# Between two layers of a fused attention and two-layer gated network: another order for the last down products, the first up products and the work beside them

## The chip, the cores and the metric

One core of a Trainium2 chip runs the whole program. TensorE (PE in the rows; its weight loads are PEld) does the matmuls, VectorE (DVE) and ScalarE (ACT) read the PSUM banks and do the elementwise work, GpSimd (POOL) does a little elementwise work in SBUF, and SyncE (SP) issues the DMAs. The metric is the time of one execution in device microseconds.

## The reference, cut to what matters

```python
x = attention(q, k, v)                  # 1536 tokens x 512
h = x @ moe_w_in                        # 512 -> 2048
x = (h * cos(h)) @ moe_w_out            # first layer, 2048 -> 512
h = x @ moe2_w_in
sp = log1p(exp(h))
out = (h * tanh(sp)) @ moe2_w_out       # second layer (the Mish gate)
```

The four weights come as 64-bit floats, and the kernel narrows them itself with integer operations.

## The kernel before, in words

Every fp32 operand of a layer's matmul is held as a high and a low part, and one 128-deep piece of a product takes three matmuls (high x high, high x low, low x high). All matmuls of the layers are 128x128 by 128x512. Tokens are three blocks j = 0, 1, 2 of 512. The output of the first layer is accumulated in ACC tiles; its two parts go to the tiles X (xh and xl), from which the second layer reads.

**First layer.** It walks over 12 stages: four groups of hidden columns times three token blocks. A stage has four up products of 12 matmuls (L180) and four down products `down(s, u)`, u = 0 to 3, of 12 matmuls (L585). Stages are numbered from 0, so stage 11 is the last one, block j = 2. A down product lands in a PSUM bank; its `add` (DVE, L594) adds the bank to ACC, which frees the bank. In the last group its `end` follows: ACT casts the high part into xh (L598) and POOL subtracts it for the low part xl (L599). Down products rotate over banks 3, 4 and 5 in this stretch.

**Between the layers** the code writes the order out by hand. Engines take their instructions in the order of the code, each waiting for what it needs.
- `do_downs(k)` issues up to two down products that are due by k. `head(k, pe)` issues the product `pe`, then the ends of the downs of the head before last, then the adds of all downs issued so far, then the low parts of gates (`later`).
- `first(f, j, bank)` is an up product of group 0 of the second layer: 12 matmuls (L698) over X of block j, first u = 0, 1, then u = 2, 3. Six of them exist, f = 0, 1 times j = 0, 1, 2.
- `gated(...)` is ACT's Mish from the bank (L675) and ACT's cast of the high part (L668); the low part (DVE, L669) comes with the next unit.
- `tsum(i, part)`, i = 0 to 3, makes sums of token blocks from ACC for the later groups (which compute some products by sums of blocks): part 0 is the sum (DVE, L737), part 1 the high part (ACT, L756), part 2 the low part (DVE, L737). They are 128x1024, or two of 128x512. `tsum(3, 1)` and `tsum(3, 2)` overwrite X of block 1, u = 0, 1.
- `chunk(h, c, ...)` narrows and splits one 128x512 weight piece: x (ACT, L123), a, b, c (DVE, L127, L130, L133), s the high part (ACT, L141), l the low part (DVE, L144). `wsums(1, p)` makes sums of the weights of group 1: parts 0 to 3 on DVE (L156), 4 on ACT (two, L162), 5 on DVE (two, L164). `wload` (L108) issues the DMA of a piece into one of two staging buffers, and waits for `c` of the piece that was there.
- `down2(0, j, u)` is a down product of group 0 of the second layer: 6 matmuls (L713). Its bank goes to ACC by an ACT copy (L723). In order, down2(0, 0, 0) has bank 4, then 5, 6, 3, and for j = 1: 4, 7, 5, 3.
- `unit(pe, post, side)` issues `pe`, then `side`, then the waiting low parts of gates, then `post`.

After that stretch a loop runs over the groups h = 1 to 7; its first product (`m1`) is six matmuls of L698.

In the kernel before the order of PE in this stretch is: first(0,0), first(1,0), down(11,0), down(11,1), first(0,1), down(11,2), first(1,1), down(11,3), four down2 of j = 0, first(0,2), one down2 of j = 1, first(1,2), three down2 of j = 1, then the loop. The first layer's last stage but one ends with down(10,3), just ahead of it.

Of the kernel before, what the change touches and what calls it, by code (L numbers as in the profile page):

```python
# [20 lines left out]
def kernel(  # L21
# [78 lines left out]
    def wload(l, g, c):  # L100
        st = wst.tile([128, 512], I64 if wide else F32, tag="wst", name="wst")
        if l == 0:
            src, r = wsrc[0][c // KD], 128 * (c % KD)
            ap = src[r:r + 128, g * GW:(g + 1) * GW] if c < KD else src[g * GW + r:g * GW + r + 128, :]
            nc.sync.dma_start(out=st, in_=ap)
        elif c < 2:
            ap = wsrc[1][0][256 * c:256 * c + 256, g * HW:(g + 1) * HW].rearrange("(k p) n -> p k n", p=128)
            nc.sync.dma_start(out=st.rearrange("p (k n) -> p k n", k=2), in_=ap)  # L108
        else:
            r = g * HW + 128 * (c - 2)  # L110
            nc.sync.dma_start(out=st, in_=wsrc[1][1][r:r + 128, :])
        wstage[l, g, c] = st
# [422 lines left out]
    def layers():  # L535
        with ExitStack() as es:
# [42 lines left out]
            def down(s, u):  # L579
                l, g, j = stages[s]  # L580
                ps = dbank()[:, 0:TB]
                mm = [(SLOT[4 * (g % 2) + 2 + a][:, 512 * f + 128 * u:512 * f + 128 * u + 128], G[s, f][e])
                      for f in range(GF) for a, e in PASS]
                for n, (x, y) in enumerate(mm):
                    nc.tensor.matmul(ps, lhsT=x, rhs=y, start=(n == 0), stop=(n == len(mm) - 1))  # L585
                if u == 0 and g == 0:
                    ACC[l, j] = ap.tile([128, KD * TB], F32, tag="acc", name="acc")
                acc = ACC[l, j][:, TB * u:TB * u + TB]

                def add():  # L590
                    if g == 0:
                        nc.scalar.copy(acc, ps)
                    else:
                        nc.vector.tensor_tensor(out=acc, in0=acc, in1=ps, op=ALU.add)  # L594

                def end():
                    hi, lo = (y[:, u, TB * j:TB * j + TB] for y in X)
                    nc.scalar.copy(hi, acc)  # L598
                    nc.gpsimd.tensor_tensor(out=lo, in0=acc, in1=hi.bitcast(F32), op=ALU.subtract)  # L599

                return [add, end] if g == NG - 1 else [add]

# [11 lines left out]
            def do_downs(k):  # L614

                for _ in range(2):
                    if downs and downs[0][0] <= k:
                        add, *end = down(*downs.pop(0)[1:])
                        adds.append(add)
                        ends[1].extend(end)  # L620
# [50 lines left out]
            def gated(h, f, j, ps, plus=None):  # L671
                g = tmp("gg")
                if plus is not None:
                    nc.vector.tensor_tensor(out=g, in0=ps, in1=plus, op=ALU.add)  # L674
                nc.scalar.activation(out=g, in_=ps if plus is None else g, func=AF.Mish)  # L675
                keep(h, f, j, g)
# [27 lines left out]
            def down2(h, j, u, d0=0, d1=DM, side=()):  # L704
                w = SLOT[slots(h)[1]]
                stay = (j, u) in STAY
                ps = (BANK[STAY[j, u]] if stay else dbank())[:, 0:d1 - d0]
                mm = [(G[1, h, f, j][a][:, 128 * u:128 * u + 128], w[:, 1024 * e + 512 * f + d0:1024 * e + 512 * f + d1])
                      for f in range(HG) for a, e in PASS]

                def pe():
                    for n, (x, y) in enumerate(mm):
                        nc.tensor.matmul(ps, lhsT=x, rhs=y, start=(n == 0 and (h == 0 or not stay)),  # L713
                                         stop=(n == len(mm) - 1 and (h == NH - 1 or not stay)))

                def post():
                    if u == 0 and h == 0:
                        ACC[1, j] = ap.tile([128, KD * TB], F32, tag="acc", name="acc")
                    acc = ACC[1, j][:, DM * u + d0:DM * u + d1]
                    if stay and h < NH - 1:  # L720
                        return
                    if h == 0 or stay:
                        nc.scalar.copy(acc, ps)  # L723
                    else:
                        nc.vector.tensor_tensor(out=acc, in0=acc, in1=ps, op=ALU.add)  # L725
                    if h == NH - 1:
                        r0 = TB * j + 128 * u
                        nc.sync.dma_start(out=out[r0:r0 + 128, d0:d1], in_=acc)

                unit(pe, post, side)  # L730
# [10 lines left out]
            def tsum(i, part):  # L741

                x, y = (ACC[0, j].rearrange("p (r n) -> p r n", r=2) for j in range(2))
                at, u, v = ((x[:, 0], y[:, 0], x[:, 0]), (y[:, 1], y[:, 1], x[:, 0]),
                            (y[:, 0], y[:, 1], y[:, 0]), (x[:, 1], x[:, 1], y[:, 1]))[i]
                if part == 0:
                    sub(at, u, v)
                    return
                dst = [(at, DST[i])]
                if i == 2:  # L750
                    dst = [(at[:, TB * k:TB * k + TB], GS[8 + k]) for k in range(2)]
                elif i == 3:
                    dst = [(at.rearrange("p (k n) -> p k n", k=2), DST[i])]
                for f, (hi, lo) in dst:
                    if part == 1:
                        nc.scalar.copy(hi, f)  # L756
                    else:
                        sub(lo, f, hi.bitcast(F32))

            def w(fn, *a):  # L760
                return lambda: fn(*a)

            def chunk(h, c, *parts):

                return [w(wnarrow, 1, h, c, "xabc".index(p)) if p in "xabc" else w(wsplit, 1, h, c, "sl".index(p))
                        for p in parts]

            def head(k, pe=None):

                if pe:  # L770
                    pe()
                now = later[:]
                later.clear()
                do_ends()
                g = cos_gate(*st.pop(k - 1)) if k - 1 in st else None
                do_adds()
                if g is not None:
                    made(k, k - 1, split(g))
                for op in now:
                    op()  # L780

            def first(f, j, bank):
                return lambda: plain(0, f, j, BANK[bank])

            for c in range(2):
                wload(1, 1, c)
            do_downs(NT1)
            head(NT1, first(0, 0, 0))
            gate.update(n=0, of=8)
            gated(0, 0, 0, BANK[0])  # L790
            head(NT1 + 1, first(1, 0, 1))
            tsum(0, 0)
            tsum(0, 1)
            gated(0, 1, 0, BANK[1])
            do_downs(NT1 + 1)
            head(NT1 + 2)
            tsum(2, 0)
            tsum(2, 1)
            for op in chunk(1, 0, *"xabcs"):
                op()  # L800
            do_downs(NT1 + 2)
            head(NT1 + 3, first(0, 1, 2))
            tsum(1, 0)
            tsum(0, 2)
            gated(0, 0, 1, BANK[2])
            for op in chunk(1, 0, "l") + chunk(1, 1, "x", "a", "b"):
                op()
            do_downs(NT1 + 3)
            head(NT1 + 4, first(1, 1, 0))
            tsum(3, 0)  # L810
            tsum(2, 2)
            gated(0, 1, 1, BANK[0])
            tsum(3, 1)
            for op in chunk(1, 1, "c", "s"):
                op()
            do_downs(NT1 + 4)
            head(NT1 + 5)
            tsum(1, 1)
            tsum(3, 2)
            down2(0, 0, 0, side=[w(tsum, 1, 2)])  # L820
            down2(0, 0, 1, side=chunk(1, 1, "l"))
            head(NT1 + 6)
            down2(0, 0, 2, side=[w(wsums, 1, 0, tmp), w(wsums, 1, 1, tmp)])
            down2(0, 0, 3, side=[w(wsums, 1, 2, tmp), w(wsums, 1, 3, tmp), w(wsums, 1, 4, tmp)])
            unit(first(0, 2, 1), w(gated, 0, 0, 2, BANK[1]), [w(wsums, 1, 5, tmp)])
            down2(0, 1, 0)
            wload(1, 2, 0)
            unit(first(1, 2, 2), w(gated, 0, 1, 2, BANK[2]))
            down2(0, 1, 1)
            wload(1, 2, 1)  # L830
            down2(0, 1, 2)
            down2(0, 1, 3, side=chunk(2, 0, "x"))

            for h in range(1, NH):
# [116 lines left out]
```

## Time and profile before

| | |
|---|---|
| median of 3 runs | 632.39 us (631.22 to 634.14) |
| the profiled execution | 632.21 us, its span 630.5 us |
| PE busy | 618.8 us, 98% of the span, 3048 matmuls |
| DVE busy | 505.2 us, 80% |
| ACT busy | 337.9 us, 54% |
| POOL busy | 104.4 us, 17% |
| granted TensorE clock | 1.00 over the span |

The span is the part of the time that the profiler sees; 1.7 us lie around it. Times in rows are microseconds from the span's start. The last products of the first layer begin at about 354 us, and the loop of the second layer begins at 402.75 us. In rows of the timeline the duration of a matmul (0.39) overlaps the next one's start; the distance of starts is what a matmul costs.

### The profile page before, as it was taken

The numbers are of one execution on the slowest core, as the hardware profiler recorded it, in microseconds if no ns is written. First come the engines' busy times: TensorE is split into PE (matmuls) and PEld (weight loads), VectorE is DVE, ScalarE is ACT, GpSimd is POOL, SyncE is SP. The second block draws the span as 40 slices with busy tenths as digits, with TensorE's granted clock in tenths as the row PEclk, the third lists the DMA queues.
The fourth block names the chain that finished last, engine by engine and source line by source line (L and its number), as shares of the span: only waits on it lengthen the run. The fifth ranks groups of instructions, "written<-read, shape, count | busy, mean of one in ns | idle before, by whom it ended". The sixth has DMA issues, their size and how long they took to land.

```text
span 630.5 us, 8778 instructions
## 1 busy us (share of the span) xinstructions
PE 618.8 (98%) x3048; PEld 504.8 (80%) x3049; DVE 505.2 (80%) x1036; ACT 337.9 (54%) x727; POOL 104.4 (17%) x196
## 2 busy tenths in 40 slices
PE   9899999999999999999999997999999999999998
PEld 4678778888888888888888885888888888888886
DVE  4699886599789888888889969577888888888653
ACT  4699887567555444444455464554444444444330
POOL 4588967000000000000002225000000000000000
PEclk9999999999999999999999999999999999999999
DMA  9979842021232111112111101113131313031004
GB/s 186 194 177 231 170 117 68 1 67 68 68 105 97 55 57 58 65 67 69 67 68 51 50 19 49 34 34 101 33 101 33 101 33 101 33 101 35 0 18 183
DMA packets 56458, 49.88 MB, mean 79 GB/s; under 512 B 44270, under 2 KB 44526, under 8 KB 56174
## 3 DMA queue, kind: packets, MB, share of 16 engines
q1 hardware_dynamic: 56414, 49.32, 27.8%
q8 instruction: 24, 0.39, 0.3%
q14 instruction: 20, 0.16, 0.1%
HBM read 45.57 MB, written 3.15 MB: 77 GB/s over the span
## 4 chain that ended last, share of the span: by engine, by line
PE 87%; POOL 5%; DVE 2%; ACT 2%; DMA 2%; issue 1%; SPq 1%; POOLq 0%; ACTq 0%
PE bank L180 21%; PE bank L713 20%; PE bank L585 19%; PE bank L698 18%; PE bank L251 10%; POOL pn L251 3%; DMA vn<-in_v_dram 2%; POOL vb L251 1%; DVE acc L737 1%; POOL xl L599 1%; POOL ws L144 1%; ACT gg L675 0%; DVE gl L669 0%; ACT gh L668 0%; DVE ws L144 0%
## 5 line engine op out<-in xcount | busy, mean ns | idle before, releaser
L180 PE MATMUL bank<-xh,ws 128*128 128x512 f32 x384 | 127.0, 392 | 0.0
L585 PE MATMUL bank<-gh,ws 128*128 128x512 f32 x384 | 125.7, 390 | 0.0
L713 PE MATMUL bank<-ws,gh 128*128 128x512 f32 (+1 forms) x388 | 118.9, 388 | 1.4 <-DVE acc L594 1.4
L698 PE MATMUL bank<-xh,ws 128*128 128x512 f32 x272 | 91.5, 390 | 0.0
L713 PEld LDWEIGHTS bank<-ws,gh 128*128 128x128 f32 x388 | 72.5, 188 | 17.1 <-DVE acc L594 2.3
L180 PEld LDWEIGHTS bank<-xh,ws 128*128 128x128 f32 x384 | 72.1, 188 | 15.6 <-DVE gg L569 0.7
L585 PEld LDWEIGHTS bank<-gh,ws 128*128 128x128 f32 x384 | 72.1, 188 | 15.0
L561 ACT ACTIVATE n<-bank,b_quarter 128x512 int32<-128x512 f32 x48 | 32.9, 686 | 79.7 <-PE bank L180 79.6
L713 PE MATMUL bank<-ws,gl 128*128 128x512 f32 (+1 forms) x194 | 75.2, 388 | 0.0
L180 PE MATMUL bank<-xl,ws 128*128 128x512 f32 x192 | 74.8, 390 | 0.0
L585 PE MATMUL bank<-gl,ws 128*128 128x512 f32 x192 | 74.8, 390 | 0.0
L141 ACT CAST ws<-wx 128x512 fp32r<-128x512 f32 x64 | 39.7, 621 | 51.3 <-DVE wx L133 51.1
L599 POOL TENSOR_TENSOR xl<-acc,xh 128x512 fp32r<-128x512 f32 x12 | 21.0, 1758 | 264.5 <-ACT xh L598 257.5
L669 DVE TENSOR_TENSOR gl<-gg,gh 128x512 fp32r<-128x512 f32 x48 | 33.2, 692 | 37.7 <-ACT gh L668 37.7
L698 PEld LDWEIGHTS bank<-xh,ws 128*128 128x128 f32 x272 | 51.1, 188 | 10.5
L251 POOL TENSOR_TENSOR pn<-pb,rs 128x256 f32<-128x256 f32 (+3 forms) x120 | 53.8, 470 | 18.7 <-ACT pb L251 6.2
L698 PE MATMUL bank<-xl,ws 128*128 128x512 f32 x136 | 53.2, 391 | 2.1 <-POOL xl L599 2.1
L725 DVE TENSOR_TENSOR acc<-acc,bank 128x512 f32<-128x512 f32 (+1 forms) x71 | 47.4, 674 | 8.5 <-PE bank L713 8.5
L562 DVE SCALAR_TENSOR_TENSOR r<-n,bank 128x512 f32<-128x512 int32 x48 | 32.9, 685 | 22.9 <-ACT n L561 22.9
L133 DVE SCALAR_TENSOR_TENSOR wx<-wst,wx 128x512 int32<-128x512 int32 x64 | 45.0, 704 | 1.5
L130 DVE SCALAR_TENSOR_TENSOR wx<-wst,wx 128x512 int32<-128x512 int32 x64 | 44.6, 697 | 1.9
L675 ACT ACTIVATE gg<-gg 128x512 f32<-128x512 f32 x28 | 17.7, 633 | 51.2 <-DVE gg L674 51.2
(100 smaller groups left out, 1092.2 us busy)
## 6 DMA issues: line engine op xcount, KB each, us to landing
wst<-in_moe_w_in_dram SPq DMA_DIRECT2D x32, 512.0 KB
wst<-in_moe_w_out_dram SPq DMA_DIRECT2D x32, 512.0 KB
kn<-in_k_dram SPq DMA_DIRECT2D x16, 192.0 KB
qn<-in_q_dram SPq DMA_DIRECT2D x16, 192.0 KB
vn<-in_v_dram SPq DMA_DIRECT2D x16, 192.0 KB
out_dram<-acc SPq DMA_DIRECT2D x11, 256.0 KB
vb<-in_v_dram SPq DMA_DIRECT2D x2, 960.0 KB
vt<-in_v_dram SPq DMA_DIRECT2D x32, 18.8 KB
```

The lines of the kernel that those rows point to most:

```text
L130: nc.vector.scalar_tensor_tensor(out=xi, in0=word[:, :, 0], scalar=29, in1=xi, op0=ALU.logical_shift_right, op1=ALU.bitwise_or)
L133: nc.vector.scalar_tensor_tensor(out=xi, in0=word[:, :, 1], scalar=-2 ** 31, in1=xi, op0=ALU.bitwise_and, op1=ALU.bitwise_or)
L141: nc.scalar.copy(hi, x)
L180: nc.tensor.matmul(ps, lhsT=SLOT[4 * (g % 2) + a][:, 512 * c + 128 * f:512 * c + 128 * f + 128], rhs=X[e][:, c, TB * j:TB * j + TB], start ...
L251: todo[phase].append(lambda: fn(*a, **kw))
L561: nc.scalar.activation(out=n, in_=h, func=AF.Identity, scale=1.0 / TWO_PI, bias=b_quarter)
L562: nc.vector.scalar_tensor_tensor(out=r, in0=n, scalar=-C1, in1=h, op0=ALU.mult, op1=ALU.add)
L585: nc.tensor.matmul(ps, lhsT=x, rhs=y, start=(n == 0), stop=(n == len(mm) - 1))
L669: later.append(lambda: nc.vector.tensor_tensor(out=lo, in0=g, in1=hi.bitcast(F32), op=ALU.subtract))
L698: nc.tensor.matmul(ps, lhsT=u, rhs=v, start=start and n == 0, stop=stop and n == len(mm) - 1)
L713: nc.tensor.matmul(ps, lhsT=x, rhs=y, start=(n == 0 and (h == 0 or not stay)), stop=(n == len(mm) - 1 and (h == NH - 1 or not stay)))
L725: nc.vector.tensor_tensor(out=acc, in0=acc, in1=ps, op=ALU.add)
```

## The change

Up to here the down products of stage 11 stand one at a time between up products. The change issues them two at a time: (11,0) and (11,1) after first(0,0), and (11,2) and (11,3) after first(1,0). The other four `first` products follow, and only then the eight down2 of group 0, with nothing between them. The tsum steps keep their order by data but are spread otherwise; all narrowing and splitting of group 1's two weight pieces and all wsums now stand beside first(1,2) and the down2, and the wloads of group 2 behind them. The low parts of (11,2) and (11,3) go from POOL to DVE.

```diff
--- before.py
+++ after.py
@@ -596,7 +596,8 @@
                 def end():
                     hi, lo = (y[:, u, TB * j:TB * j + TB] for y in X)
                     nc.scalar.copy(hi, acc)
-                    nc.gpsimd.tensor_tensor(out=lo, in0=acc, in1=hi.bitcast(F32), op=ALU.subtract)
+                    eng = nc.vector if j == NBLK - 1 and u >= 2 else nc.gpsimd
+                    eng.tensor_tensor(out=lo, in0=acc, in1=hi.bitcast(F32), op=ALU.subtract)
 
                 return [add, end] if g == NG - 1 else [add]
 
@@ -784,51 +785,48 @@
 
             for c in range(2):
                 wload(1, 1, c)
+            def some(*ops):
+                for op in ops:
+                    op()
+
             do_downs(NT1)
             head(NT1, first(0, 0, 0))
             gate.update(n=0, of=8)
             gated(0, 0, 0, BANK[0])
-            head(NT1 + 1, first(1, 0, 1))
+            do_downs(NT1 + 2)
+            head(NT1 + 1)
             tsum(0, 0)
+            head(NT1 + 2, first(1, 0, 1))
+            tsum(2, 0)
+            gated(0, 1, 0, BANK[1])
+            do_downs(NT1 + 4)
+            head(NT1 + 3)
+            tsum(1, 0)
             tsum(0, 1)
-            gated(0, 1, 0, BANK[1])
-            do_downs(NT1 + 1)
-            head(NT1 + 2)
-            tsum(2, 0)
             tsum(2, 1)
-            for op in chunk(1, 0, *"xabcs"):
-                op()
-            do_downs(NT1 + 2)
-            head(NT1 + 3, first(0, 1, 2))
-            tsum(1, 0)
+            head(NT1 + 4, first(0, 1, 2))
+            gated(0, 0, 1, BANK[2])
+            tsum(3, 0)
+            head(NT1 + 5, first(1, 1, 0))
+            gated(0, 1, 1, BANK[0])
             tsum(0, 2)
-            gated(0, 0, 1, BANK[2])
-            for op in chunk(1, 0, "l") + chunk(1, 1, "x", "a", "b"):
-                op()
-            do_downs(NT1 + 3)
-            head(NT1 + 4, first(1, 1, 0))
-            tsum(3, 0)
+            tsum(1, 1)
             tsum(2, 2)
-            gated(0, 1, 1, BANK[0])
             tsum(3, 1)
-            for op in chunk(1, 1, "c", "s"):
-                op()
-            do_downs(NT1 + 4)
-            head(NT1 + 5)
-            tsum(1, 1)
+            head(NT1 + 6, first(0, 2, 1))
+            gated(0, 0, 2, BANK[1])
+            tsum(1, 2)
             tsum(3, 2)
-            down2(0, 0, 0, side=[w(tsum, 1, 2)])
-            down2(0, 0, 1, side=chunk(1, 1, "l"))
-            head(NT1 + 6)
-            down2(0, 0, 2, side=[w(wsums, 1, 0, tmp), w(wsums, 1, 1, tmp)])
-            down2(0, 0, 3, side=[w(wsums, 1, 2, tmp), w(wsums, 1, 3, tmp), w(wsums, 1, 4, tmp)])
-            unit(first(0, 2, 1), w(gated, 0, 0, 2, BANK[1]), [w(wsums, 1, 5, tmp)])
-            down2(0, 1, 0)
+            unit(first(1, 2, 2), w(gated, 0, 1, 2, BANK[2]), chunk(1, 0, *"xabcs"))
+            down2(0, 0, 0, side=chunk(1, 0, "l") + chunk(1, 1, "x"))
+            down2(0, 0, 1, side=chunk(1, 1, "a", "b"))
+            down2(0, 0, 2, side=chunk(1, 1, "c", "s"))
+            down2(0, 0, 3, side=[w(wsums, 1, p, tmp) for p in range(3)])
+            down2(0, 1, 0, side=[w(wsums, 1, p, tmp) for p in range(3, 5)])
             wload(1, 2, 0)
-            unit(first(1, 2, 2), w(gated, 0, 1, 2, BANK[2]))
-            down2(0, 1, 1)
+            down2(0, 1, 1, side=chunk(1, 1, "l"))
             wload(1, 2, 1)
-            down2(0, 1, 2)
+            down2(0, 1, 2, side=[w(wsums, 1, 5, tmp)])
             down2(0, 1, 3, side=chunk(2, 0, "x"))
 
             for h in range(1, NH):
```

## Rows read from the trace of the kernel before

**Rows 1.** The page: busy time by engine, share of the span, instructions.
```profile
PE 618.8 (98%) x3048; PEld 504.8 (80%) x3049; DVE 505.2 (80%) x1036; ACT 337.9 (54%) x727; POOL 104.4 (17%) x196
```

**Rows 2.** Waits, 360 to 400 us: waiter, releaser, total us, times, longest.
```profile
PEld bank L698 <- POOL xl L599: 3.0, 2, 2.1
...
PEld bank L713 <- DVE acc L594: 2.3, 2, 1.5
```

**Rows 3.** Timeline of PE: start, us, engine, line, operation [idle before <- releaser].
```profile
359.86 0.39 PE L698 MATMUL bank<-xh,ws 128*128 128x512 f32 x1
...
381.62 0.62 PE L713 MATMUL bank<-ws,gh 128*128 128x512 f32 x2
...
402.75 0.39 PE L698 MATMUL bank<-xh,ws 128*128 128x512 f32 x1
```

**Rows 4.** Busy us (instructions) of PE, PEld, DVE, ACT, POOL; clock, DMA share, GB/s.
```profile
376.00:381.60 5.60, 5.60 (x26) 4.66 (x25) 5.60 (x5) 4.45 (x8) 3.28 (x2) 1.00 0.30 95
381.60:388.00 6.40, 4.97 (x21) 3.46 (x20) 6.37 (x11) 2.06 (x3) 0.00 (x0) 1.00 0.00 0
388.00:394.50 6.50, 4.39 (x18) 2.99 (x17) 6.47 (x9) 3.30 (x6) 5.70 (x2) 1.00 0.27 81
394.50:400.00 5.50, 5.50 (x25) 4.51 (x24) 2.01 (x4) 3.81 (x7) 0.00 (x0) 1.00 0.00 0
```

**Rows 5.** Timeline of DVE.
```profile
366.01 2.33 DVE L737 TENSOR_TENSOR acc<-acc 128x1024 f32<-128x1024 f32 x1
368.26 0.67 DVE L594 TENSOR_TENSOR acc<-acc,bank 128x512 f32<-128x512 f32 x1
...
374.20 0.43 DVE L127 TENSOR_SCALAR wx<-wx 128x512 int32<-128x512 int32 x1 [1.76 <-ACT wx L123]
374.66 0.69 DVE L130 SCALAR_TENSOR_TENSOR wx<-wst,wx 128x512 int32<-128x512 int32 x1
...
387.47 0.69 DVE L669 TENSOR_TENSOR gl<-gg,gh 128x512 fp32r<-128x512 f32 x1
388.07 1.22 DVE L737 TENSOR_TENSOR xl<-acc,xh 128x1024 fp32r<-128x1024 f32 x1
389.21 1.22 DVE L737 TENSOR_TENSOR ws<-acc,ws 128x1024 fp32r<-128x1024 f32 x1
...
390.95 0.42 DVE L156 TENSOR_TENSOR n<-wx 128x256 f32<-128x256 f32 x1
```

**Rows 6.** The chain that ended last, in order of time: start, us, what.
```profile
388.21 4.28 POOL xl L599
```

**Rows 7.** Timeline of POOL.
```profile
353.56 1.30 POOL L599 TENSOR_TENSOR xl<-acc,xh 128x512 fp32r<-128x512 f32 x1 [4.71 <-ACT xh L598]
...
365.97 3.53 POOL L599 TENSOR_TENSOR xl<-acc,xh 128x512 fp32r<-128x512 f32 x2 [6.29 <-ACT xh L598]
```

**Rows 8.** Timeline of ACT.
```profile
378.31 0.67 ACT L123 ACTIVATE wx<-wst 128x512 f32<-128x512 f32 x1
378.88 0.60 ACT L598 CAST xh<-acc 128x512 fp32r<-128x512 f32 x1
379.39 0.59 ACT L675 ACTIVATE gg<-bank 128x512 f32<-128x512 f32 x1
380.01 0.62 ACT L668 CAST gh<-gg 128x512 fp32r<-128x512 f32 x1
...
402.07 0.66 ACT L123 ACTIVATE wx<-wst 128x512 f32<-128x512 f32 x1
```

**Rows 9.** Timeline of SP: from the start of one wload to the end of the next.
```profile
376.15 11.24 SPq L108 DMA_DIRECT2D wst<-in_moe_w_in_dram  x2
```

**Rows 10.** Columns as rows 4, just after the second of these two issues.
```profile
389.00:390.00 1.00, 1.00 (x6) 0.83 (x5) 1.00 (x2) 0.70 (x3) 1.00 (x1) 1.00 0.78 297
390.00:391.00 1.00, 0.89 (x4) 0.38 (x3) 1.00 (x3) 0.97 (x2) 1.00 (x1) 1.00 0.00 0
```

**Rows 11.** Timeline of PEld: the weight load of first(0,2)'s second matmul.
```profile
389.12 0.19 PEld L698 LDWEIGHTS bank<-xl,ws 128*128 128x128 f32 x1
```

## The prediction

> **What bounds the kernel now.** I read the page first: PE is busy 98% of the span and the matmuls are the same before and after, so a change of order can only win back what PE stands still [rows 1]. Then the waits of the stretch that the diff reorders: PE's weight loads wait twice for a DVE add that frees a bank, and twice for POOL's low part xl [rows 2]. These columns don't give the loss, because the drawn ends of matmuls overlap. The starts do. From first(0,0) at 359.86 to down2(0,0,0) at 381.62 stand 8 products, 96 matmuls: 21.76 us, 0.2267 each. PE loses nothing there. From 381.62 to the loop at 402.75 stand 72 matmuls (eight down2 of 6, two first of 12), worth 16.32 us, and they take 21.13. **The loss is 4.81 us**, 0.76% of the time, and the most that the change can win here [rows 3].
>
> What makes the waits is DVE. It is busy 18.44 of 18.50 us from 376.0 to 394.5, and idle for over half of the 5.5 us after that [rows 4]. So the adds of (11,2) and (11,3) come late: down(11,3) ended at 381.62, DVE's operation behind its add starts only at 387.47 [rows 5], and down2(0,0,3) needs that bank. ACT's cast of (11,2) waits behind a cast of weights that DVE hasn't narrowed, and POOL's low part, begun at 388.21, takes 4.28 us [rows 6]; the same subtraction took 1.30 elsewhere [rows 7]. The clock is granted at 1.00 in these stretches, the 2.4 GHz level, and costs nothing [rows 4].
>
> **Prices.** Start to start when packed, DVE takes 0.60 for a 128x512 subtraction or add and 1.14 for a 128x1024 one; of narrowing, a takes 0.46 and b and c, of one form, some 0.71 each, a wsums part 0.42 to 0.45 [rows 5]. ACT takes 0.57 for x, 0.51 for a cast with work behind it (0.62 to its end), 0.62 from Mish to its cast [rows 8]; a copy out of a bank is counted as a cast, 0.6, and a 1024 high part as two, 1.0. An add follows its product by 0.24: down(11,0) ended at 359.86 + 36 x 0.2267 = 368.02, its add began at 368.26 [rows 3, 5].
>
> **The new order on PE, if nothing waits.** first(0,0) starts at 359.86 as before. Each product of 12 costs 2.72: down(11,0), (11,1) run from 362.58 to 368.02, first(1,0) to 370.74, down(11,2), (11,3) to 376.18, first(0,1) to 378.90, first(1,1) to 381.62, first(0,2) to 384.34, first(1,2) to 387.07, the eight down2 (1.36 each) to 397.94. I now ask of each what it needs.
>
> *Banks.* down(11,3) takes bank 3 back at 373.46; the add of (11,0) can start at 365.54. The first three down2 and the fourth need adds that can now run at 368.3, 373.7 and 376.4, over 10 us ahead of 387.07. Both bank waits of before go.
>
> *First(0,2)* needs all of X block 2. Casts of (11,0), (11,1) follow their adds at once, and POOL, with (10,2), (10,3) from 365.97 as before [rows 7], has both low parts by 368.6 + 2 x 1.30 = 371.2; at the worst row, 4.28 each, by 377.2 [rows 6]. (11,2), (11,3) are new on DVE. No row shows this subtraction there; the same shape and operands cost 0.60 (L669), a 1024 sum beside POOL lost 1.1 over its 1.22 [rows 5]. I take 0.60, since POOL has nothing left by then. On DVE stand from 376.42: add (11,3), a gate's low part, tsum(1,0), then these two: done at 376.42 + 4 x 0.60 + 1.14 = 379.96. PE reads them at its 8th and 11th matmul, from 383.2: 3.2 us of cover.
>
> *The DVE queue behind that* is the chain with the least room. From 376.42 to the end of tsum(3,2) it holds eight 128x512 operations (4.80) and five 1024 ones (5.70): 386.92. What they wait for from ACT is earlier: tsum(1,1) ends near 384.0, tsum(3,1), behind first(1,1)'s gate, near 385.0. Then a, b, c of the first piece, 1.88: 388.80. ACT meanwhile stands at s, which waits for c, and behind s are queued the gate of first(1,2), x of the second piece and only then the copy that frees bank 4: 388.82 + 0.51 + 0.62 + 0.51 + 0.57 + 0.60 = 391.6. **down2(0,1,0) needs bank 4 at 392.5: 0.9 us of room.** I cost it at 0. If the chain runs later, each us beyond 0.9 is a us lost.
>
> *Weights.* DVE goes on: two gates' low parts and l (to about 391.2, waiting for ACT), a, b, c of the second piece (393.1), four wsums (394.9), l, and with ACT's two casts between, wsums 5 to 396.8. The loop's second product wants them at 399.30: 2.5 us of room. This is 8 us of DVE work (two pieces of 1.88 + 0.60, four wsums of 0.45, two low parts of 0.60). Before, it stood ahead of and beside first(0,2); now it stands where DVE was half idle.
>
> *DMAs.* SP's two wloads wait for c, so they go out at 388.8 and 393.1, where before the first began at 376.15 and the second was out by 387.39; nothing else is in SP's queue [rows 9]. The second had moved its data by 390.0, 2.6 us later [rows 10]. The first is read by ACT's x at 402.07 before, so near 397.3 now [rows 8]: it lands 5.9 us ahead. The second lands at 395.7 and is read units later. Cost 0.
>
> **Sum:** 4.81 us won, nothing paid. The profiled execution's 632.21 becomes 627.4; it stands 0.18 below the median shown, so 627.6 there. I say 627.5.
>
> **The rivals.**
> 1. *Bank 4 is freed late.* Place: down2(0,1,0), behind ACT's s. For it: 0.9 us is 6% of a chain of some 20 steps, 376.4 to 391.6, summed by hand, and ACT's order puts four things ahead of the copy. Against: the steps are packed rows of the same shapes. With the chain 2 us late, 1.1 is lost: 628.5; with 4 us, 630.5.
> 2. *POOL and DVE hold each other up at the start of that chain.* A 1024 sum that began 0.04 us after POOL's subtraction took 2.33 instead of 1.22, and POOL's two took 3.53 instead of 2.6 [rows 5, 7]. If (11,0) and (11,1) take 4.28 each, POOL ends at 368.6 + 8.6 = 377.2, past 376.42; DVE's low part at 377.0 can then be held for as long as POOL's own 1.30, which is 0.4 more than the room: 627.9. Against: DVE has only 2.9 us of such work between 368.9 and 373.7, then waits for PE; and an add from a bank took 0.67 beside POOL [rows 5].
> The Trainium skill, SBUF — State Buffer, "Who interferes with whom", says that a DVE instruction with two SBUF inputs and a GpSimd instruction that reads SBUF exclude each other, the second being blocked until the first ends. By that rule POOL's last operation is blocked by at most one DVE operation each time, the two end by about 368.6 + 2 x (1.30 + 1.14) = 373.5, and the rival falls. The 4.28 of [rows 6] is more than one such block, so the trace doesn't bear that out as the whole of it.
> 3. *First(0,2) is held by tsum(3,1)*, which writes X block 1 and now stands close ahead of it in the code: PE would wait from 381.62 to 385.03, 3.4 lost, 630.8. Against: before, the second matmul's weight load ran at 389.12, while tsum(3,2) was still writing xl from 388.07 for 1.22 [rows 5, 11].
> 4. *The other side: DVE stays the bound.* DVE was full up to 394.5 [rows 4], and the change gives it 1.20 us more (two low parts). If what it moves behind first(0,2) merely returns as waits at the down2, the loss stays and grows: 633.4. It decides once the chain is 0.9 + 4.8 = 5.7 us later than summed; for a loss beyond 0.5% it would take 8.9. For it: DVE without a gap for 18 us. Against: 8 us of it are not due before 397.
>
> **Chances.** 0.5% (3.2 us) is about what can be told from no change here. Full gain 0.73 (626.5 to 628.5 with the spread of runs); rival 1, 0.11, half of it beyond 629.2; rival 2, 0.05; rival 3, 0.05; rival 4, 0.06, most of it 632 to 636. By the cases faster is 0.73 + 0.05 + half of 0.11, 0.83; the runs shown spread by 2.9 us, which can hide so small a gain, and I take 0.75; same 0.20; slower 0.05. The range takes in rivals 1 to 3: 626.3 to 630.9.
>
> **What would show it.** In the profile after: PE without idle time from 359.9, first(0,2) starting near 381.6, the first down2 near 387.1, the loop near 397.9; no PE wait for L594 or L599; POOL with ten L599 and DVE with two of them near 379. Rival 1 would show as a wait of L713 for ACT L723 near 392.5; rival 2 as POOL's last L599 ending after 376; rival 3 as first(0,2) waiting for L756; rival 4 as the loop starting after 402.75, and DVE's chain past 392. The prediction is wrong if the loop starts early and the gain is lost behind it: there PE has no wait to lose now, and the phase of weights and gates to PE is nearly the same.

## The result, and the profile after

The changed kernel takes 626.66 us in the median of 4 executions (626.19 to 627.27), the kernel before 632.22: ratio 0.9901, 95% interval 0.9881 to 0.9921. The forecast was 627.5 with a range of 626.3 to 630.9; it was faster, as forecast, but the ratio puts the time at 0.9901 x 632.39 = 626.1, just below the range. How far below is uncertain: the interval of the ratio gives 624.9 to 627.4, and the quotient of the two medians, 0.9912, gives 626.8, inside the range. The profiled execution took 626.57 us, its span 624.8.

The timeline of PE, after (first(0,0), the first down2, the loop):

```profile
359.01 0.39 PE L699 MATMUL bank<-xh,ws 128*128 128x512 f32 x1
...
386.21 0.61 PE L714 MATMUL bank<-ws,gh 128*128 128x512 f32 x2
...
397.09 0.39 PE L699 MATMUL bank<-xh,ws 128*128 128x512 f32 x1
```

From first(0,0) to the loop it is 38.08 us, which is 168 matmuls at 0.2267 and not a hundredth more; before it was 402.75 - 359.86 = 42.89 [rows 3]. So 4.81 us are won in the stretch, as in the sum. Everything in it starts 0.85 us earlier than summed, because first(0,0) does: that part lies ahead of the change. The tail from the loop to the end of the span is 227.71 against 227.75.

Busy time in the windows of [rows 4], with the same columns, after:

```profile
376.00:381.60 5.60, 5.60 (x26) 4.65 (x25) 5.60 (x8) 2.45 (x4) 0.00 (x0) 1.00 0.00 0
381.60:388.00 6.40, 6.40 (x30) 5.29 (x29) 6.33 (x10) 4.28 (x7) 0.00 (x0) 1.00 0.01 1
388.00:394.50 6.50, 6.50 (x30) 5.38 (x29) 5.82 (x12) 5.45 (x11) 0.00 (x0) 1.00 0.45 130
394.50:400.00 5.50, 5.50 (x26) 4.56 (x25) 2.93 (x5) 3.53 (x7) 0.00 (x0) 1.00 0.10 37
```

DVE (third busy column) is still full to 388, but PE (first) no longer waits for it. POOL has nothing here, and the last two windows have the DVE work that was put off.

### The profile page after: what moved, and what is told of

Same layout as the page of the kernel before. It is cut to its first block, busy times and chain, and to the rows that moved or that the text cites. A ratio compares the mean times of both kernels' runs of the same rounds, so it can differ in the third digit from the quotient of the medians.

```text
span 624.8 us, 8776 instructions
## 1 busy us (share of the span) xinstructions
PE 616.6 (99%) x3049; PEld 504.3 (81%) x3049; DVE 503.8 (81%) x1038; ACT 338.2 (54%) x727; POOL 97.3 (16%) x194
## 4 chain that ended last, share of the span: by engine, by line
PE 92%; DMA 2%; DVE 2%; ACT 1%; POOL 1%; SPq 0%; issue 0%
PE bank L180 21%; PE bank L714 21%; PE bank L585 21%; PE bank L699 19%; PE bank L251 10%; DMA vn<-in_v_dram 1%; DMA wst<-in_moe_w_in_dram 1%; POOL pn L251 1%; DVE pb L251 1%; DVE ks L251 0%; DVE rs L251 0%; DVE kx L251 0%; ACT kx L251 0%; POOL ws L144 0%; ACT pt L251 0%
## 5 line engine op out<-in xcount | busy, mean ns | idle before, releaser
L600 POOL TENSOR_TENSOR xl<-acc,xh 128x512 fp32r<-128x512 f32 x10 | 14.0, 1420 | 249.1 <-ACT xh L598 249.1
```

## Experiments

"Stretch" is the time from first(0,0) to the loop in the profile of a run; without any wait it is 38.08. The ratio is against the executions of the kernel before taken with that run. "Low clock" counts executions whose granted TensorE clock, averaged over the span, is below 0.9985; in these it is 0.997, in five of them (four of the run with eight idle operations, one with the low parts on DVE alone) 0.995. The first row takes all executions of the kernel before whose clock is on record.

| kernel | stretch, us | median, us | ratio (95%) | low clock |
|---|---|---|---|---|
| before, all 71 executions | 42.89 | mean 632.66 | | 24 of 71 |
| before against itself | 42.84 | 632.06 | 0.9988 (0.9977 to 1.0) | 2 of 12 |
| after | 38.08 | 626.66 | 0.9901 (0.9881 to 0.9921) | 0 of 4 |
| weights put off alone | 38.08 | 627.35 | 0.9916 (0.9898 to 0.9934) | 0 of 4 |
| after, weights early | 38.08 | 627.56 | 0.9917 (0.9897 to 0.9937) | 0 of 4 |
| after, weights early, low parts on POOL | 38.08 | 627.32 | 0.9917 (0.9900 to 0.9934) | 0 of 4 |
| after, low parts on POOL | 38.08 | 627.35 | 0.9916 (0.9899 to 0.9932) | 0 of 4 |
| low parts on DVE alone | 42.54 | 632.27 | 0.9996 (0.9983 to 1.001) | 7 of 10 |
| wsums put off alone | 44.48 | 632.79 | 1.0002 (0.9987 to 1.0018) | 3 of 10 |
| after, 2 idle DVE operations | 38.44 | 628.14 | 0.9931 (0.9915 to 0.9946) | 0 of 6 |
| after, 5 | 41.83 | 630.42 | 0.9959 (0.9944 to 0.9975) | 4 of 10 |
| after, 8 | 43.58 | 633.07 | 1.0007 (0.9996 to 1.0019) | 12 of 12 |

**The kernel before against itself.** No edit.

> The kernel before, unchanged, against itself. The question is the part of the gain that lies ahead of the change: in the profile after, first(0,0) starts at 359.01 instead of 359.86, 0.85 us sooner, though every instruction up to there is the same. If this is spread from run to run of the attention stage, first(0,0) starts here anywhere from 358.5 to 361.5 while the stretch from it to the loop stays at 42.9, and the ratio is 1.000 with an interval of some 0.002 to either side. If the old program is slower there as such, first(0,0) starts at 359.9 or later again.

first(0,0) started at 359.88, the stretch took 42.84. In the nine profiles of kernels that differ only behind it (all but those with idle operations), first(0,0) started anywhere from 359.01 (after) to 360.39 (weights put off alone): the 0.85 us is spread of the attention stage. The first layer's first product has it already: it starts from 103.46 (after) to 104.85 (weights put off alone), 255.5 us ahead of first(0,0) in each. The ratio of the program to itself was 0.9988, so comparisons here are uncertain by some 0.1%. But the executions of the kernel before fall into two groups: 632.09 us in the mean of 47 at the full clock, 633.77 in 24 at the low one.

**The weights put off, nothing else.**

```diff
-            for op in chunk(1, 0, *"xabcs"):
...
-            for op in chunk(1, 0, "l") + chunk(1, 1, "x", "a", "b"):
...
-            unit(first(0, 2, 1), w(gated, 0, 0, 2, BANK[1]), [w(wsums, 1, 5, tmp)])
-            down2(0, 1, 0)
+            unit(first(0, 2, 1), w(gated, 0, 0, 2, BANK[1]), chunk(1, 0, *"xabcs"))
+            down2(0, 1, 0, side=chunk(1, 0, "l") + chunk(1, 1, "x"))
...
-            unit(first(1, 2, 2), w(gated, 0, 1, 2, BANK[2]))
-            down2(0, 1, 1)
+            unit(first(1, 2, 2), w(gated, 0, 1, 2, BANK[2]), chunk(1, 1, "a", "b", "c", "s"))
+            down2(0, 1, 1, side=[w(wsums, 1, p, tmp) for p in range(5)])
...
-            down2(0, 1, 2)
+            down2(0, 1, 2, side=chunk(1, 1, "l") + [w(wsums, 1, 5, tmp)])
```

> The kernel before with one part of the change alone: the narrowing and splitting of group 1's weights and all wsums stand beside first(0,2), first(1,2) and the last three down2; PE's order and POOL's low parts stay as before. Theory 1, a full DVE queue makes adds and low parts late: without the 8 us of weights DVE does both adds within 0.3 us of the downs' ends, the stretch from first(0,0) to the loop takes 38.1 to 39.0 instead of 42.9, and the time falls by 4 to 4.8 us. Theory 2, it is PE's order (too little room between a down product and what reads it): the two bank waits and the wait for xl stay, 41.5 or more, under 1.4 us won.

Stretch 38.08, the whole 4.81. DVE's adds and POOL's low parts, from the timelines of this run:

```profile
376.91 0.69 DVE L594 TENSOR_TENSOR acc<-acc,bank 128x512 f32<-128x512 f32 x1 [1.09 <-PE bank L585]
...
382.35 0.69 DVE L594 TENSOR_TENSOR acc<-acc,bank 128x512 f32<-128x512 f32 x1 [1.25 <-PE bank L585]
```
```profile
382.43 1.31 POOL L599 TENSOR_TENSOR xl<-acc,xh 128x512 fp32r<-128x512 f32 x1 [4.21 <-ACT xh L598]
387.18 1.28 POOL L599 TENSOR_TENSOR xl<-acc,xh 128x512 fp32r<-128x512 f32 x1 [3.44 <-ACT xh L598]
```

DVE now waits for PE before both adds, and POOL's 4.28 us are 1.31. PE's old order is enough if DVE's queue is short: theory 2 falls. The time fell by 632.96 - 627.31 = 5.65 us in the mean of the executions taken with it, more than the 4 to 4.8 expected; the part beyond the stretch is taken up below.

**The new order with the weights early**, first with the two low parts on DVE, then with them on POOL, so that only the order of products and sums is new.

```diff
             gated(0, 1, 0, BANK[1])
+            some(*chunk(1, 0, *"xabcs"))
...
             tsum(3, 0)
+            some(*chunk(1, 0, "l"), *chunk(1, 1, "x", "a", "b"))
...
             tsum(3, 1)
+            some(*chunk(1, 1, "c", "s"))
...
-            unit(first(1, 2, 2), w(gated, 0, 1, 2, BANK[2]), chunk(1, 0, *"xabcs"))
+            unit(first(1, 2, 2), w(gated, 0, 1, 2, BANK[2]), chunk(1, 1, "l"))
...
+            down2(0, 0, 0, side=[w(wsums, 1, 0, tmp), w(wsums, 1, 1, tmp)])
+            down2(0, 0, 1, side=[w(wsums, 1, 2, tmp), w(wsums, 1, 3, tmp), w(wsums, 1, 4, tmp)])
+            down2(0, 0, 2, side=[w(wsums, 1, 5, tmp)])
```
```diff
-                    eng = nc.vector if j == NBLK - 1 and u >= 2 else nc.gpsimd
+                    eng = nc.gpsimd
```

> The kernel after with the weights back where they stood before in the code: a, b, c of the first piece behind the gate of first(1,0), the rest beside first(0,1) to the down2. PE's order, the tsum order and the two low parts on DVE are the new ones. By a sum of rows DVE then holds 2.5 us more ahead of tsum(3,2), which ends near 388.8 on the clock of the profile after, the copy that frees bank 4 near 389.5, ahead of the 391.65 at which down2(0,1,0) wants it: stretch 38.1 to 38.6. If the weights' place alone decides (theory 1 at its strongest), the waits come back: 41 or more.

> PE's new order and the new tsum order, with the weights early and the low parts of (11,2), (11,3) on POOL: nothing of the change but the order of products and sums. POOL's low parts can begin near 379.2 on the clock of the weights-early run, in the packed part of DVE, and first(0,2) reads them at 383.6 and 384.2. With 4.28 us each, as before, 3.5 us are lost: stretch 41.6. With one DVE operation to wait for each, as the run with both on POOL showed (2.15 us), nothing: 38.1.

Both: 38.08. DVE was nearly as full as before with the weights early (18.07 and 18.31 us busy of the 18.50 from 376.0 to 394.5, against 18.43), and PE did not wait. So theory 1 at its strongest falls too: a full DVE queue costs nothing if what PE waits for stands early enough in it, or its reader comes late enough. The new order issues (11,2) one product earlier and (11,3) two, and puts the down2 that want their banks behind four up products. first(0,2), which reads their low parts, stands as far behind down(11,3) in the order as before (two up products in place of four down2 of half the length). There it is the writers that moved: with the low parts on POOL, DVE runs both adds from 375.21, ahead of the narrowing of the second piece, ACT casts from 377.85, ahead of the weight cast behind which the first of them stood before, and POOL needs 4.01 for the two:

```profile
375.21 1.48 DVE L594 TENSOR_TENSOR acc<-acc,bank 128x512 f32<-128x512 f32 x2
...
378.54 4.01 POOL L600 TENSOR_TENSOR xl<-acc,xh 128x512 fp32r<-128x512 f32 x2 [7.45 <-ACT xh L598]
```

The two parts of the change, weights off and new order, each win all of the 4.81; together they win it once.

**The two low parts**, back on POOL in the kernel after (the one-line edit above), and the other way round on DVE in the kernel before.

> The kernel after with the low parts of (11,2) and (11,3) back on POOL. The first can run near 374.8 while DVE is idle, 1.3 us; the second is ready at 376.9 when DVE is packed and may take the 4.28 of before, to 381.2; first(0,2) reads it at 383.0. So no wait of PE, stretch 38.1, and DVE's chain between 0.1 us later and 1.2 us earlier. If POOL was the limit as such, first(0,2) waits for POOL and the stretch takes 39.5 to 42.

> The kernel before with one line of the change: the low parts of (11,2) and (11,3) on DVE. Theory 1 (the full DVE queue): the low part of (11,2) waits on DVE for ACT's cast, done at 388.13, and the add of (11,3) is queued behind it, so down2(0,0,3) starts some 1.9 us later than 387.61; first(0,2) no longer waits for POOL's 4.28 us. Sum: stretch 42.0 to 42.9 instead of 42.89, under 1 us won. If POOL's lateness is what costs, 40.0 to 40.5.

With both on POOL the stretch stays 38.08. POOL's timeline there, and DVE's two sums of that moment:

```profile
375.84 1.29 POOL L600 TENSOR_TENSOR xl<-acc,xh 128x512 fp32r<-128x512 f32 x1 [4.19 <-ACT xh L598]
377.99 2.15 POOL L600 TENSOR_TENSOR xl<-acc,xh 128x512 fp32r<-128x512 f32 x1 [0.85 <-ACT xh L598]
377.77 3.45 DVE L738 TENSOR_TENSOR acc<-acc 128x1024 f32<-128x1024 f32 x2
```

The second began 0.22 us after a 1024 sum of DVE with two SBUF inputs had started at 377.77, and waited out that one sum: 2.15, not 4.28. The two sums took 3.45 where packed ones take 2.36 (1.14 + 1.22): the second waited in its turn. Alone on the kernel before, the same line moves the wait instead of removing it:

```profile
389.66 0.73 PE L714 MATMUL bank<-ws,gh 128*128 128x512 f32 x2 [3.00 <-DVE acc L594]
...
393.83 0.50 PE L699 MATMUL bank<-xl,ws 128*128 128x512 f32 x1 [0.23 <-DVE xl L600]
...
388.32 0.69 DVE L600 TENSOR_TENSOR xl<-acc,xh 128x512 fp32r<-128x512 f32 x1 [1.20 <-ACT xh L598]
388.93 0.68 DVE L594 TENSOR_TENSOR acc<-acc,bank 128x512 f32<-128x512 f32 x1
```

The wait for xl shrinks to 0.23, and the one for bank 3 grows from 1.11 to 3.00, since the add stands in DVE's queue behind a low part that waits for ACT's cast. This line is no part of the gain.

**The wsums put off alone.**

```diff
-            down2(0, 0, 2, side=[w(wsums, 1, 0, tmp), w(wsums, 1, 1, tmp)])
-            down2(0, 0, 3, side=[w(wsums, 1, 2, tmp), w(wsums, 1, 3, tmp), w(wsums, 1, 4, tmp)])
-            unit(first(0, 2, 1), w(gated, 0, 0, 2, BANK[1]), [w(wsums, 1, 5, tmp)])
-            down2(0, 1, 0)
+            down2(0, 0, 2)
+            down2(0, 0, 3)
+            unit(first(0, 2, 1), w(gated, 0, 0, 2, BANK[1]))
+            down2(0, 1, 0, side=[w(wsums, 1, p, tmp) for p in range(3)])
...
-            unit(first(1, 2, 2), w(gated, 0, 1, 2, BANK[2]))
-            down2(0, 1, 1)
+            unit(first(1, 2, 2), w(gated, 0, 1, 2, BANK[2]), [w(wsums, 1, 3, tmp), w(wsums, 1, 4, tmp)])
+            down2(0, 1, 1, side=[w(wsums, 1, 5, tmp)])
```

> The kernel before with only the sums of weights (wsums) put off behind first(0,2); the narrowing stays. These 3 us of DVE stand behind the adds in DVE's queue, so the two bank waits stay (down2(0,0,3) near 387.6); only POOL's two low parts find DVE less busy and end up to 0.5 us sooner. Stretch 42.2 to 42.7. If any 3 us off DVE would do, 38.1 to 40.

The waits for banks and for POOL stayed as they were (0.33, 1.08, 1.65, 0.44), and not even POOL's end moved: nothing that DVE waits for stood between the old place in the code and the new one, so DVE ran the first three wsums at the same moments. The first of them began at 390.95 before [rows 5] and here, with first(0,0) 0.39 later, at

```profile
391.33 0.42 DVE L156 TENSOR_TENSOR n<-wx 128x256 f32<-128x256 f32 x1
```

So nothing was won, where 0.2 to 0.7 us had been expected, and the stretch of the profiled execution was 1.6 us longer. Its windows (columns as in [rows 4]) show why:

```profile
394.00:395.00 1.00, 0.66 (x3) 0.57 (x4) 0.57 (x1) 0.00 (x0) 0.29 (x1) 1.00 0.00 0
395.00:396.00 1.00, 1.00 (x5) 0.78 (x4) 0.00 (x0) 0.86 (x2) 0.00 (x0) 0.58 0.00 0
396.00:397.00 1.00, 1.00 (x4) 0.81 (x3) 0.61 (x1) 0.36 (x1) 0.00 (x0) 0.50 0.00 0
397.00:398.00 1.00, 1.00 (x4) 0.81 (x3) 0.42 (x2) 0.47 (x1) 0.00 (x0) 0.50 0.00 0
398.00:399.00 1.00, 1.00 (x4) 0.75 (x4) 0.33 (x1) 1.00 (x3) 0.00 (x0) 0.72 0.00 0
399.00:400.00 1.00, 1.00 (x6) 0.80 (x5) 0.96 (x2) 0.15 (x1) 0.00 (x0) 1.00 0.00 0
```

PE works without a gap from 395, but the granted clock is 0.50, the 1.2 GHz level, for some 3.5 us. A matmul costs 0.42 there, from the starts of PE's timeline, where the usual price is 0.227. Outside 360 to 400 us the clock of this execution is 1.00. This had not been in the sum, nor in any row of before.

**Idle DVE operations ahead of the first weight piece**, in the kernel after: five, two, eight. They compute nothing that is used.

```diff
+            scr = gp.tile([128, 384], F32, tag="scr", name="scr")
+            nc.vector.memset(scr, 0.0)
+            def extra():
+                nc.vector.tensor_tensor(out=scr, in0=scr, in1=scr, op=ALU.max)
...
-            unit(first(1, 2, 2), w(gated, 0, 1, 2, BANK[2]), chunk(1, 0, *"xabcs"))
+            unit(first(1, 2, 2), w(gated, 0, 1, 2, BANK[2]), [extra] * 5 + chunk(1, 0, *"xabcs"))
```

> The kernel after with five DVE operations of 128x384 that serve nothing ahead of a, b, c of the first weight piece, about 0.47 us each, 2.35 in all. The chain that frees bank 4 (a, b, c, ACT's s, gate, x, copy) has 0.9 us of room by the sum and by the profile after (copy done at 390.76, bank wanted at 391.65). So down2(0,1,0) waits for ACT's copy by 1.4 to 1.5 us, stretch 39.5. If the room is larger than that chain says, 38.1.

> As the run with five idle DVE operations ahead of a, b, c, with two. One took 0.57 there, so 1.14 in all, less 0.89 of room: down2(0,1,0) waits 0.25, stretch 38.3 to 38.4. Theory A on the rest of the gain (0.6 us more than the 4.81 of the stretch, which the low clock after PE's waits gives in a third of the executions of the kernel before): after so short a wait no execution shows the low clock, all stand at 0.999 or 1.0, mean 627.2 + 0.3 = 627.5. Theory B, the low clock comes from something else in this order of work: a third of the executions at 0.997, as with five.

> The same with eight: 4.56 us less 0.89 of room, a wait of 3.7 at down2(0,1,0), stretch 41.7 in executions that keep the full clock, 43.4 to 43.8 in those with the low clock after it. Theory A: the low clock at least as often as with five (4 of 10); mean 631.0 to 632.6. Theory B: no more than a third of the executions, and the time follows from the wait alone, 630.9 on the mean.

The timeline of PE with five:

```profile
394.49 0.73 PE L720 MATMUL bank<-ws,gh 128*128 128x512 f32 x2 [1.82 <-ACT acc L730]
395.06 0.40 PE L720 MATMUL bank<-ws,gl 128*128 128x512 f32 x1
395.30 0.99 PE L720 MATMUL bank<-ws,gh 128*128 128x512 f32 x2
396.09 0.63 PE L720 MATMUL bank<-ws,gl 128*128 128x512 f32 x1
396.51 1.05 PE L720 MATMUL bank<-ws,gh 128*128 128x512 f32 x2
```

down2(0,1,0) waits for ACT's copy, as rival 1 had it. It should have started at 359.87 + 144 x 0.2267 = 392.5, so the wait is 2.0; a stands 389.73 - (386.03 + 0.86) = 2.84 us later than in the kernel after; the room is the difference, 0.86. (An idle operation took 0.57, not 0.47; hence 2.0 and not the 1.4 to 1.5 expected.) Then a matmul takes 396.51 - 396.09 = 0.42 instead of 0.227, and the stretch comes out 1.8 longer than the wait alone makes it: the expected 39.5 misses it. With two operations the wait is 0.36 and no execution has the low clock; with eight it is 3.7 and all twelve have it. Theory B falls. Not all came as expected: the mean is 628.10 with two, 0.6 us above the expected one, and 633.04 with eight, 0.4 us above the range expected. Against 627.22, the mean of the kernels without a wait (below), with the wait and the fall (as often as it came) added, the three doses are 0.3 to 0.5 us too slow, and where that lies is not shown. One of the ten executions with five took 631.37 at the full clock, as long as those at the low one; what held it is not shown either.

## Why the prediction came out as it did

**The stretch was right, step by step.** With 0.85 taken off for the earlier start, the summed times and the profile after agree: first down2 386.22 and 386.21, loop 397.09 and 397.09, SP's first wload 387.95 and 387.97, ACT's x of group 2 396.45 and 396.41, the last wsums, on which nothing hung, 395.95 and 395.62. DVE's chain, from its timeline after:

```profile
367.97 1.50 DVE L670 TENSOR_TENSOR gl<-gg,gh 128x512 fp32r<-128x512 f32 x1
369.39 3.64 DVE L738 TENSOR_TENSOR acc<-acc 128x1024 f32<-128x1024 f32 x2
...
375.53 0.69 DVE L594 TENSOR_TENSOR acc<-acc,bank 128x512 f32<-128x512 f32 x1 [1.90 <-PE bank L585]
...
377.87 1.29 DVE L600 TENSOR_TENSOR xl<-acc,xh 128x512 fp32r<-128x512 f32 x2
...
384.89 1.22 DVE L738 TENSOR_TENSOR xl<-acc,xh 128x1024 fp32r<-128x1024 f32 x1
386.03 0.42 DVE L127 TENSOR_SCALAR wx<-wx 128x512 int32<-128x512 int32 x1
```

tsum(3,2) ends at 386.11, summed 386.07. The room at bank 4, summed at 0.9, was measured as 0.86.

**The rivals.** Rival 1 did not come, but its place and its price were true: with idle operations PE waits there and nowhere else. Rival 2 cost nothing: POOL's four remaining operations ended at 365.12 + 5.50 = 370.62, 4.9 us ahead of the chain's first add at 375.53. Beside them DVE lost 2.1 us, as the first two lines above show (1.50 for a low part of 0.69, 3.64 for two sums of 2.36), but then still waited 1.90 us for PE.

```profile
365.12 5.50 POOL L600 TENSOR_TENSOR xl<-acc,xh 128x512 fp32r<-128x512 f32 x4 [6.28 <-ACT xh L598]
```

With the 0.85 added, POOL's end is 371.5: by the sum it was 371.2, by the rival 377.2. The rule weighed there (the Trainium skill, SBUF — State Buffer, "Who interferes with whom") had allowed 373.5, and the 2.15 us above agree with it: POOL waited for one DVE operation, and the next one of DVE for POOL. Why it waited for more in the 4.28 of [rows 6] stays open. Rivals 3 and 4 did not come; PE has no wait in the stretch, and DVE full for 12 us cost nothing.

**The step that failed** is "The clock is granted at 1.00 in these stretches, the 2.4 GHz level, and costs nothing". It was read from one execution. In 24 of 71 executions of the kernel before, the mean clock over the span is low; these take 633.77 - 632.09 = 1.68 us longer, 24/71 x 1.68 = 0.57 on the mean. The change takes away the waits and with them the low clock: none of the 20 executions of the kernels without a wait has it. The sum with this term: 4.81 + 0.57 = 5.38. Measured, over the 20 executions of the five kernels with a stretch of 38.08 (mean 627.22): 632.66 - 627.22 = 5.44, and against the full-clock executions alone 632.09 - 627.22 = 4.87, for the 4.81 of the stretch. What the first four executions of the kernel after show beyond that (626.66) is 0.6 us better than the mean of its equals; with starts of first(0,0) spread over 1.4 us and no difference in what stands ahead of it, I take it for spread, which the range's lower end, 626.3, had left too little room for; that is not shown. Over all 71 and 20 executions the ratio is 627.22/632.66 = 0.9914, or 627.0 in place of the 632.39, inside the range: that the first ratio fell 0.2 us below it is in part luck. The missing term is shown by the later runs, not by those 0.2 us. That "the runs shown spread by 2.9 us" was in part this low clock: it was named as noise, and would have been worth a question.

That PE's waits bring the low clock is shown by the three doses, in kernels that differ only in the number of idle operations. These operations are not the cause as such: the kernel before has none of them. Nor is a full DVE: with the weights early it is nearly as full as before, and none of 8 executions has the low clock. How the fall is set off is not shown, and no profile at hand shows an execution of the kernel before with it; that the term there has the same cause is argued from its size and from the run with wsums put off, whose waits are the same.

## What to carry to other kernels

A sum of packed rows along one engine's queue, set against the moment at which PE reads the result, gave the moments that PE depends on to 0.1 us; it is worth doing before any reordering. A sum that is late can be mended by taking work from the queue ahead of it, or by issuing it earlier and its reader later, and doing both wins nothing more. It doesn't even give more room everywhere: at bank 4 the kernel after has 0.9 us, the one with the weights early 360.21 + 144 x 0.2267 - (389.73 + 0.58) = 2.5. Where PE stands still, price the clock after the wait as well: look at several executions, not at one profile, and ask what a spread in the times is made of.

## What the runs showed of the hardware

After PE had stood still for 2.0 us, the granted clock fell from 1.00 to 0.50 for some 3.5 us while PE was already at work again. One profile shows this, and by the mean clock over the span it came in 4 of 10 executions; after 3.7 us in 12 of 12; after 0.36 us in none of 6. With the low parts on DVE alone, where the longest of three waits is 3.0 us, it was 7 of 10. One fall costs 1.6 to 1.8 us in the three profiles that have one, nearly as much as the 2.0 us wait that brings it. The run with eight operations, in the windows in which PE is back (columns as in [rows 4]):

```profile
396.00:397.00 1.00, 0.83 (x4) 0.70 (x5) 0.93 (x3) 0.60 (x2) 0.00 (x0) 1.00 0.06 23
397.00:398.00 1.00, 1.00 (x4) 0.82 (x3) 0.97 (x2) 0.37 (x1) 0.00 (x0) 0.57 0.00 0
398.00:399.00 1.00, 1.00 (x4) 0.71 (x3) 0.97 (x4) 1.00 (x3) 0.00 (x0) 0.50 0.34 55
```

The Trainium skill, TensorE: Matmul & The Clock Gate, "Part 1: The HAM clock gate (the "warmup" mystery)", gives 1.2 GHz as the level of an idle or cold array; the 0.50 here agrees, and it is granted while PE is busy again.

And work that was put off in the code was not put off in time where the engine had nothing to wait for in between: three wsums that moved two and three units down the code began at the same moments, counted from first(0,0), to 0.02 us.
